# q, k and v projections in 64-row halves, and one pool of 8 PSUM banks, in a transformer block scheduled by a written timetable

## The chip, the cores and the metric

The kernel runs on one core of one Trainium2 chip. The metric is the time of the device in microseconds, from one launch; it is given as the median of a few runs. A profile is one execution recorded by the hardware profiler; its span runs from the first to the last instruction of the program. The engines are called PE (TensorE, matmuls; PEld are its weight loads), DVE (VectorE), ACT (ScalarE), POOL (GpSimd) and SP (SyncE, which issues most DMAs).

## The reference

One block on x of 2048 tokens and 576 features. First a linear-memory attention with 32 heads of 18 features, in four segments of 512 tokens, then a feed-forward part of 4608 hidden features.

```python
xn = layernorm(x)
q, k, v = xn @ wq, xn @ wk, xn @ wv            # 32 heads of 18
for s in range(4):                             # 512 tokens each
    a_dot = softmax(qs @ ks.T * scale + causal_mask) @ vs
    a_mem = (phi(qs) @ M) / (phi(qs) @ z + 1e-6)   # phi(t) = t + 1 if t > 0 else exp(t)
    o = g * a_mem + (1 - g) * a_dot            # g = sigmoid(beta), one for each head
    M, z = M + phi(ks).T @ vs, z + sum(phi(ks))
h = x + o @ wo
out = h + gelu(layernorm(h) @ w1 + b1) @ w2 + b2
```

## The kernel before

The work is written as a graph of some 1,770 operations, each with an engine, a function that issues its instructions, the operations it follows, and the buffers it takes (`acq`) and uses. `Graph.add` gives every operation its place from `TIMETABLE`: a row such as `"P1Pk": "p 174 207 ..."` holds the engine letter and, for each operation of that stage and name in turn, a rank. `Graph.schedule` sorts all operations by rank, picks a buffer number for each acquired buffer with a small cost table, and then issues the operations in that order; each engine carries out its own in order, and waits are made from the data that instructions touch. So the timetable alone decides the order on every engine, and the cost table decides nothing but buffer numbers.

The stages, for segment s:

- X: load 128 tokens of x (two tiles at once from segment 1 on), layer norm on DVE (`stats`, `apply`) with the `rstd` on POOL, and a transpose to `xT` (features on partitions), on PE (`TX`) in segment 0 and by DMA (`flip`) in the others. 576 features are four blocks of 128 and one of 64.
- P: for each of the four tiles of 128 tokens, k, q and v. `proj` (line 743, matmul on line 750) makes one half of the output, 288 columns, in one PSUM bank by five matmuls whose stationary operand is a 128x128 block of `xT` and whose moving operand is 288 columns of the weights; the fifth uses 65 rows. `proj2` (matmul on line 761) makes both halves at once for k and q of the first two tiles. The halves are copied out by ACT or DVE (`copy`), k and q into a padded tile that goes to DRAM (`qkst`) and comes back transposed (`flip`), and `ek`, `rk` and `fk` make phi(k).
- M: the memory update, 32 matmuls on line 852, two additions (`macc`) and the block-diagonal copy (`mblk`).
- A: attention. For two groups of four heads, five score steps (`st`, line 1067; `st0` on line 916 in segment 0), each with 32-row matmuls into four banks at once, an `exp` of 128x2048 on ACT, causal masks on POOL or DVE (`mask`), then the weighted values (`val`, line 1093; line 948 in segment 0) with 32-column matmuls, a DVE transpose and the normalisation (`valT`, `rec`, `comb`). From segment 1 on `mem` (line 1044) reads the memory, with `memT` and `memfin` after it.
- B: the output projection (`Po`, also line 750), the residual (`hadd`), the second layer norm, and a transpose to `x2T`. h goes to DRAM and comes back later (`hc`).
- C: the first feed-forward matmul F1 with 64-row matmuls in pairs, two groups of hidden features side by side (line 1206; 1243 for segment 0, in halves of 256 tokens), copied out with the bias and put through gelu in batches, in segment 3 directly (`gelu1`).
- D: the second feed-forward matmul F2 (line 1293), 36 matmuls of 288 columns into one bank for each of eight outputs of a segment, then the residual (`oadd`) and the store.

A matmul thus comes in four shapes: full (128 rows and columns), 64-row pairs, 32-row fours and 32-column fours.

PSUM has 8 banks of 2 KB for each partition. Before, four of them are the pool `ps_c`, which nearly everything uses. The other four are at first two pairs for `proj2` (`pr`), then, once these are released, the one score tile `st`, and for F1 of segment 3 four single banks (`ps_l`). Since there is one score tile, a score step follows the exp of the score step ahead of it.

SP is a single queue in which the loads of x, of the weights (`w1g`, 576 KB each, three buffers), the stores and the transposes by DMA stand in timetable order.

Of the kernel before, what the change touches and what calls it, by code (L numbers as in the profile page):

```python
# [18 lines left out]
SWITCH = dict(act=1.35, pe=0.1)  # L19
INF = 1e9  # L20
# [276 lines left out]
}  # L297


# [108 lines left out]
def kernel(  # L408
# [12 lines left out]
    P = 128  # L421
# [1030 lines left out]
```

## Time and profile before

| | |
|---|---|
| time, median of 3 runs | 450.41 us (449.86 to 450.85) |
| span of the profiled execution | 448.2 us |
| granted PE clock in it | 1.000 |
| busy in the span: PE, DVE, ACT, POOL | 436.8, 288.7, 300.1, 182.5 us |
| DMA | 76.54 MB, mean 171 GB/s |

The profile does not give the whole time of its execution, only the span. The median of the runs is 2.2 us above it; that difference is taken for what lies around the span.

Rows of groups read: line, engine, operation, output tile <- input tiles, shapes, count | busy us, mean ns of one | idle us of the engine just ahead of them, and what ended it. Matmuls overlap, so the mean of one is its own length and not the distance to the next.

### The profile page before, as it was taken

To read this page: it belongs to the slowest core of one execution; us is meant where nothing else is said; L and a number is where in the kernel's file an instruction comes from. 1 tells how busy PE (TensorE), PEld (TensorE's weight loads), DVE (VectorE), ACT (ScalarE), POOL (GpSimd) and SP (SyncE) were. 2 spreads that over 40 slices of the span, in tenths; PEclk is the share of its full clock that TensorE was granted. 3 is DMA by queue.
4 is the path that set the end of the run, shared out by engine and by line. 5 is a ranking of instruction groups with operands and counts; after the bars stand their busy time and mean duration, and the time that the engine had idled before them with its cause. 6 is when DMAs were issued, how large, how long until landed. Compare 5 with 4: busy or idle time off the path is not lost.

```text
span 448.2 us, 11504 instructions
## 1 busy us (share of the span) xinstructions
PE 436.8 (97%) x4813; PEld 279.9 (62%) x4815; DVE 288.7 (64%) x618; ACT 300.1 (67%) x271; POOL 182.5 (41%) x305
## 2 busy tenths in 40 slices
PE   8978999999999999999999999999999999999997
PEld 4655677776676667664344766655447775445775
DVE  4989899998888877688878879966764011000011
ACT  4888889998887789776999976665766002664000
POOL 4687577447933556743534347432101011000020
PEclk9999999999999999999999999999999999999999
DMA  7799799996979958956663529515460592540020
GB/s 275 198 235 283 204 262 219 260 258 228 227 212 316 331 104 225 242 116 172 206 155 78 143 73 259 107 41 168 113 188 16 148 263 68 187 145 1 0 80 26
DMA packets 81732, 76.54 MB, mean 171 GB/s; under 512 B 59024, under 2 KB 68880, under 8 KB 81680
## 3 DMA queue, kind: packets, MB, share of 16 engines
q1 hardware_dynamic: 81392, 75.59, 61.9%
q8 instruction: 37, 0.61, 0.5%
q10 hardware_dynamic: 288, 0.22, 0.2%
q14 instruction: 15, 0.12, 0.1%
HBM read 42.63 MB, written 19.20 MB: 138 GB/s over the span
## 4 chain that ended last, share of the span: by engine, by line
PE 84%; DVE 8%; POOL 3%; DMA 2%; issue 2%; ACT 0%; SPq 0%; DVEq 0%; POOLq 0%; ACTq 0%
PE ps_c L1293 29%; PE ps_c L1206 16%; PE ps_c L750 13%; PE ps_l L1206 8%; PE ps_c L1243 7%; PE st L1067 4%; PE ps_c L1093 3%; DMA x<-in_A_x_dram 2%; PE ps_c L1044 1%; PE st L916 1%; PE ps_c L948 1%; DVE xn L687 1%; DVE e L1038 1%; DVE t L962 1%; DVE t L1047 1%
## 5 line engine op out<-in xcount | busy, mean ns | idle before, releaser
L1071 ACT ACTIVATE pt<-st 128x2048 bf16<-128x2048 f32 x60 | 112.6, 1877 | 32.1 <-PE st L1067 21.2
L1293 PEld LDWEIGHTS <-hT 128*128 128x128 bf16 x1152 | 111.0, 98 | 33.8 <-issue 5.5
L1206 PEld LDWEIGHTS <-w1g 64*128 64x128 bf16 x972 | 46.6, 94 | 56.5 <-issue 3.2
L1293 PE MATMUL ps_c<-w,hT 128*128 128x288 bf16 x576 | 78.4, 286 | 0.6 <-DVE t L1047 0.6
L1293 PE MATMUL ps_c<-w_lo,hT 128*128 128x288 bf16 x576 | 77.4, 286 | 0.2 <-issue 0.2
L1206 PE MATMUL ps_c<-xreg,w1g 64*128 64x512 bf16 x648 | 72.9, 376 | 0.0
L1305 DVE TENSOR_TENSOR ot<-ps_c,hc 128x288 bf16<-128x288 f32 x32 | 13.7, 448 | 79.1 <-PE ps_c L1293 77.9
L750 PE MATMUL ps_c<-hT,xreg 128*128 128x288 bf16 (+1 forms) x440 | 60.6, 286 | 1.7 <-DVE qk_pad L599 1.4
L1082 POOL TENSOR_SCALAR_AFFINE_SELECT pt<-pt 128x512 bf16<-128x512 bf16 x59 | 42.3, 728 | 39.6 <-ACT pt L1071 39.5
L1211 ACT ACTIVATE hT<-ps_l,b_col 128x512 bf16<-128x512 f32 x36 | 22.7, 684 | 46.2 <-PE ps_l L1206 46.2
L750 PEld LDWEIGHTS <-xreg 128*128 128x128 bf16 (+1 forms) x440 | 40.9, 97 | 16.3 <-issue 5.1
L1279 POOL TENSOR_TENSOR hc<-hc,b_bc 128x576 f32<-128x576 f32 x11 | 14.4, 1309 | 83.1 <-DMA hc<-hd 83.1
L919 ACT ACTIVATE pt<-st 128x2048 bf16<-128x2048 f32 x20 | 37.6, 1878 | 4.7 <-PE st L916 4.3
L1221 DVE TENSOR_SCALAR hT<-ps_c,b_col 128x512 bf16<-128x512 f32 x45 | 32.4, 743 | 11.9 <-PE ps_c L1206 11.9
L1243 PE MATMUL ps_c<-xreg,w1g 64*128 64x256 bf16 x648 | 38.3, 270 | 0.3 <-DVE t L1053 0.3
L1206 PE MATMUL ps_l<-xreg,w1g 64*128 64x512 bf16 x324 | 35.1, 376 | 0.0
L1243 PEld LDWEIGHTS <-w1g 64*128 64x128 bf16 x648 | 30.5, 94 | 6.3 <-issue 2.9
L1226 ACT ACTIVATE hT<-hT 128x8192 bf16<-128x8192 bf16 (+2 forms) x6 | 31.8, 5321 | 0.3 <-DVE hT L1221 0.2
L1219 ACT ACTIVATE hT<-ps_c,b_col 128x512 bf16<-128x512 f32 x27 | 17.9, 685 | 16.5 <-PE ps_c L1206 16.3
L676 POOL TENSOR_SCALAR ln<-ln 128x1 f32<-128x1 f32 x32 | 8.9, 277 | 43.8 <-DVE ln L673 42.5
L1067 PE MATMUL st<-qk 32*128 32x512 bf16 (+3 forms) x384 | 23.8, 301 | 0.0
L750 PE MATMUL ps_c<-wt_o,oT 128*128 128x288 bf16 x160 | 22.7, 286 | 0.0
(114 smaller groups left out, 583.8 us busy)
## 6 DMA issues: line engine op xcount, KB each, us to landing
w1g<-in_B_w_dram SPq DMA_DIRECT2D x42, 576.0 KB, 4.6
qkd<-qk_pad SPq DMA_DIRECT2D x15, 512.0 KB, 3.2
hd<-h SPq DMA_DIRECT2D x16, 288.0 KB, 3.8
hc<-hd SPq DMA_DIRECT2D x16, 288.0 KB, 4.1
w_lo<-in_B_w_dram SPq DMA_DIRECT2D x3, 864.0 KB, 5.5
w<-in_B_w_dram SPq DMA_DIRECT2D x3, 864.0 KB, 7.6
xb<-in_A_x_dram SPq DMA_DIRECT2D x16, 144.0 KB, 3.5
x2d<-xn SPq DMA_DIRECT2D x14, 160.0 KB, 2.0
```

The costliest lines, as they stand in the source:

```text
L750: nc.tensor.matmul(out=c.t[:, 0:HALF], lhsT=xTb.t[0:kk, k, ts], rhs=wt[0:kk, hf, k, :], start=(k == 0), stop=(k == 4))
L919: ex = add(ps, {"act": 1.88}, lambda e: nc.scalar.activation(out=pt.t[:], in_=st.t[:], func=ACT.Exp, scale=scale), [sc], pt, [st], table=" ...
L1067: nc.tensor.matmul(out=st.t[:, i, off:off + n_], lhsT=qk[rows, 1, kt * P:(kt + 1) * P], rhs=qk[rows, 0, kt * P:L], start=True, stop=True, ...
L1071: ex = add(ps, {"act": 1.88}, lambda e, st=st, pt=pt: nc.scalar.activation(out=pt.t[:], in_=st.t[:], func=ACT.Exp, scale=scale), [sc], pt, ...
L1082: nc.gpsimd.affine_select(out=blk, in_=blk, pattern=[[0, 4], [1, P]], compare_op=ALU.is_ge, fill=0.0, base=0, channel_multiplier=-1)
L1206: nc.tensor.matmul(out=cc[w].t[:], lhsT=w1.t[rows, k, q, :], rhs=x2T[s].t[rows, k, :], start=(k == 0), stop=(k == ND - 1))
L1211: ready_f[f + w] = [add(pf - 12, {"act": 0.68}, lambda e, f=f, w=w, cc=cc: nc.scalar.activation(out=hT[:, :, f + w, :], in_=cc[w].t[:].rea ...
L1219: nc.scalar.activation(out=dst, in_=src, func=ACT.Identity, bias=b)
L1221: nc.vector.tensor_scalar(out=dst, in0=src, scalar1=b, scalar2=None, op0=ALU.add)
L1226: ge = add(2.9, {"act": 0.42 * (f1 - f0) + 0.2}, lambda e, f0=f0, f1=f1: nc.scalar.activation(out=hT[:, :, f0:f1, :], in_=hT[:, :, f0:f1, ...
L1243: nc.tensor.matmul(out=cc[w].t[:, q * 2 * P:(q + 1) * 2 * P], lhsT=w1.t[rows, k, q, :], rhs=x2T[s].t[rows, k, ts], start=(k == 0), stop=(k ...
L1293: nc.tensor.matmul(out=c.t[:, 0:HALF], lhsT=hT[:, tl // 2, f, (tl % 2) * P:(tl % 2 + 1) * P], rhs=w2_c[ch][:, f - ch * WCH, hf * HALF:(hf ...
```

## The change

1. `proj` keeps only the output projection. q, k and v go through the new `proj_pair`, which makes both output halves of a tile as three operations: the first part (`Pk`, `Pq`, `Pv`), a fence (`pass`) and the second part (`Rk`, `Rq`, `Rv`). In the first part rows 0 to 63 of the array work on output half 0 and rows 64 to 127 on output half 1, each into its own bank, in five steps; in the second part they change banks and do the remaining four steps. The fence is a memset of a 128x1 tile on DVE or POOL that waits for the last two matmuls of the first part, and the second part's first matmul waits for it. Where the two parts stand next to each other on PE, `schedule` marks them `fused`: then there is no fence, and both halves are made whole by ten matmuls of 128 rows.
2. For this the last 64 features stand twice: x has 640 columns in DRAM, the last 64 repeated, `apply` works on 640, and the fifth block of each weight holds output half 0 in rows 0 to 63 and output half 1 in rows 64 to 127. The memset of the tails of `xn` goes.
3. All 8 PSUM banks are one tile, `bank`. A score step and a `proj2` take four or two neighbouring banks, everything else one; `pick` prefers banks 4 to 7 for single ones.
4. `mem` may be issued as four 32-column matmuls (`alt`), where it stands next to operations of that shape.
5. Buffers: `pt` 5 instead of 4, `t1` 2 instead of 1, `w1` 4 instead of 3. The scratch for dynamic DMA is set to 4096.
6. The whole timetable is new, with some numbers of the cost table. Among the new rows 13 of the 44 `pass` operations are on DVE and 31 on POOL; those of fused pairs issue nothing.

```diff
 class Slots:
-    def __init__(self, tiles):
-        self.tiles = tiles
+    def __init__(self, tiles, whole=None, pref=0):
+        self.tiles, self.whole, self.pref = tiles, whole, pref
...
+    def pick(self, t0):
+        free, w = self.home.free, self.width
+        if self.want is not None:
+            return self.want
+        if w > 1:
+            return min(range(0, len(free), w), key=lambda g: max(free[g:g + w]))
+        ready = [i for i in range(len(free)) if free[i] <= t0] if self.home.pref else []
+        return min([i for i in ready if i >= self.home.pref] or ready or range(len(free)), key=lambda i: free[i])
...
     def schedule(self):
...
+        on_pe = [o for o in order if o.eng == "pe"]
+        for a, b in zip(on_pe, on_pe[1:]):
+            if a.mate is b:
+                a.fused = b.fused = True
...
+            elif op.alt is not None:
+                was = next((o.mode for o in reversed(on_pe[:n]) if o.mode), None)
+                then = next((o.table for o in on_pe[n + 1:] if o.alt is None), None)
+                if was == op.alt or (was != op.mode and then == op.alt):
+                    op.mode = op.alt
...
-    c_s = slots(4, [P, 512], "ps_c", F32, psum)
-    pair_pool, score_pool = ExitStack(), ExitStack()
-    pr_pool = pair_pool.enter_context(tc.tile_pool(name="pairs", bufs=1, space=PSUM))
-    pr_s = slots(2, [P, 2, 512], "pr", F32, pr_pool)
-    st_s = Slots([None])
...
+    banks_all = psum.tile([P, 8, 512], F32, name="bank")
+    c_s = Slots([banks_all[:, j, :] for j in range(8)], banks_all, 4)
...
-        def proj(prio, xTb, tl, nm, hf, after, c):
+        def proj_pair(prio, xTb, tl, nm, after, cc):
             ts = slice(tl * P, (tl + 1) * P)
             wt = wts[nm]
 
+            def rows(w, hf, k, start, stop):
+                r = slice(64 * w, 64 * w + 64)
+                return nc.tensor.matmul(out=cc[hf].t[:, 0:HALF], lhsT=xTb.t[r, k, ts], rhs=wt[r, hf, k, :], start=start, stop=stop, skip_group_check=True)
+            last, passed = [], []
+
+            def fn_f(e):
+                if a.fused:
+                    return
+                passed.append(VEC[e].memset(mark_of[e][:], 0.0))
+                for to in last:
+                    tc.add_manual_dep(passed[0].ins, to.ins.name, SYNC, reason="the two halves of the rows change banks")
+
+            def fn_a(e):
+                if a.fused:
+                    return
+                for k in range(KT):
+                    last[:] = [rows(0, 0, k, k == 0, False), rows(1, 1, k, k == 0, False)]
+
+            def fn_b(e):
+                if not b.fused:
+                    for k in range(KT - 1):
+                        for w in range(2):
+                            i = rows(w, 1 - w, k, False, k == KT - 2)
+                            if k == 0 and w == 0:
+                                tc.add_manual_dep(i.ins, passed[0].ins.name, SYNC, reason="the two halves of the rows change banks")
+                    return
+                for hf in range(2):
+                    for k in range(KT):
+                        nc.tensor.matmul(out=cc[hf].t[:, 0:HALF], lhsT=xTb.t[:, k, ts], rhs=wt[:, hf, k, :], start=(k == 0), stop=(k == KT - 1))
+            a = add(prio, {"pe": 0.613}, fn_a, list(after) + w_ok[nm], cc, [xTb], table="rows64", name="P" + nm)
+            f = add(prio, {"dve": 0.07, "pool": 0.13}, fn_f, [a], name="pass")
+            b = add(prio, {"pe": 0.49}, fn_b, [a, f], None, cc + [xTb], table="rows64", name="R" + nm)
+            a.mate, f.fence = b, a
+            return b
...
-                    for hf in range(2):
-                        c = Buf(c_s)
-                        a = proj(PE_P[s] + 0.001 * tl if s > 1 else p0, xT, tl, nm, hf, [xn_ok[s, tl]], c)
+                    cc = [Buf(c_s), Buf(c_s)]
+                    a = proj_pair(PE_P[s] + 0.001 * tl if s > 1 else p0, xT, tl, nm, [xn_ok[s, tl]], cc)
...
-                st, pt = Buf(st_s), Buf(pt_s)
+                st, pt = Buf(c_s, width=4), Buf(pt_s)
...
-        A_x=a["A_x"],
+        A_x=np.concatenate([a["A_x"], a["A_x"][:, :, 512:]], axis=2),
```

Two rows of the timetable, before and after (ranks run to 1773 before and to 1815 after):

```diff
-    "P2Pk": "p 342 366 411 422 463 529 572 562",
+    "P2Pk": "p 372 424 533 587",
+    "P2Rk": "p 381 433 538 591",
+    "P2pass": "g373 g432 d652 d425 g483 d510 g534 g542 d503 d588 g606 g517",
```

More of the change, by code (lines that the diff above doesn't have):

```diff
@@ L336, in __init__ @@
         self.behind, self.bulk, self.bias, self.tag = None, False, {}, ""
+        self.alt, self.mate, self.fused, self.fence, self.mode = None, None, False, None, table
 class Graph:
@@ L371, in schedule @@
             done.add(op)
+            if op.fence is not None and op.fence.fused:
+                op.start, op.end = op.fence.end, -1.0
+                continue
             t0 = max([free[e]] + [self.seen(a, e) for a in op.after])
             for b in op.acq:
-                b.n = min(range(len(b.home.free)), key=lambda i: b.home.free[i]) if b.want is None else b.want
-                t0 = max(t0, b.home.free[b.n])
-                assert t0 < INF, (op.tag, op.name)
-                b.home.free[b.n] = INF
+                b.n = b.pick(t0)
+                for j in range(b.n, b.n + b.width):
+                    t0 = max(t0, b.home.free[j])
+                    assert t0 < INF, (op.tag, op.name)
+                    b.home.free[j] = INF
             if op.bulk:
@@ L380, in schedule @@
             c = op.cost[e]
-            kind = op.table or ("full" if e == "pe" else None)
+            if op.fused:
+                c = 0.0 if op.mate is not None else FUSED
+            kind = op.mode if e == "pe" else op.table
             if kind is not None and kind != table.get(e):
@@ L396, in schedule @@
                 if b.left == 0:
-                    b.home.free[b.n] = b.end + 0.2
+                    for j in range(b.n, b.n + b.width):
+                        b.home.free[j] = b.end + 0.2
         return order
@@ L506 @@
     mark = const.tile([1, 1], F32, name="mark")
+    mark_of = {e: const.tile([P, 1], F32, name=f"mark_{e}") for e in ("dve", "pool")}
     b1_col = const.tile([P, NF], F32, name="b1_col")
@@ L544 @@
     hd = tc.dram_tile([S, D], F32, name="hd")
-    late_s = Slots([None] * 4)
-    def to_late():
-        if late_s.tiles[0] is None:
-            score_pool.close()
-            pool = ctx.enter_context(tc.tile_pool(name="late_ps", bufs=1, space=PSUM, reuse_waits="tile"))
-            late_s.tiles[:4] = [pool.tile([P, 512], F32, name=f"ps_l{j}") for j in range(4)]
     eps_parts = []
@@ L608, in fn @@
                 for i in range(n):
-                    nc.tensor.matmul(out=acq[i // 2].t[:] if acq else wst.t[:, 0, :], lhsT=warm[:, 0:P], rhs=warm[:], start=True, stop=True)
+                    nc.tensor.matmul(out=acq[i // 2].t[:] if acq else wst.t[:], lhsT=warm[:, 0:P], rhs=warm[:], start=True, stop=True)
             return add(-9, {"pe": cost}, fn, after, acq, use, name="warm")
@@ L612, in build @@
         wprev = warm_up(4, 1.72, [wprev], [Buf(c_s), Buf(c_s)])
-        wprev = add(-9, {"pe": 0.5}, lambda e: [nc.tensor.matmul(out=wst.t[:, 0, :], lhsT=warm[:, 0:P], rhs=warm[:], start=True, stop=True) for _ in range(2)],
+        wprev = add(-9, {"pe": 0.5}, lambda e: [nc.tensor.matmul(out=wst.t[:], lhsT=warm[:, 0:P], rhs=warm[:], start=True, stop=True) for _ in range(2)],
                     [wprev], wst, name="warm")
-        z_xn = memset(-9, "pool", 0.5, *[t[:, D:XW] for t in xn_s.tiles])
         half_ok = memset(-9, "dve", 0.1, mhalf[:], val=-0.5)
@@ L741, in stage_X, with proj, fn @@
                     xn_ok[s, 2 * j] = xn_ok[s, 2 * j + 1] = [prev]
-        def proj(prio, xTb, tl, nm, hf, after, c):
+        def proj(prio, xTb, tl, hf, after, c):
+            ts = slice(tl * P, (tl + 1) * P)
+            def fn(e):
+                for k in range(KT):
+                    nc.tensor.matmul(out=c.t[:, 0:HALF], lhsT=xTb.t[:, k, ts], rhs=wts["o"][:, hf, k, :], start=(k == 0), stop=(k == 4))
+            return add(prio, {"pe": 0.62}, fn, list(after) + w_ok["o"], c, [xTb], name="Po")
@@ L933, in mask @@
                                                     base=0, channel_multiplier=-1)
[L934 removed]
+                    masks[u] = add(ps, {"dve": 0.87, "pool": 1.17}, mask, [ex, tri_ok], None, [pt], name="mask")
                     masks[u].bias = {"dve": MASK_BIAS}
@@ L1041, in stage_A, with mem @@
                 t2s[g] = t2
-                def mem(e, g=g, c=c, eb=eb):
-                    nc.tensor.matmul(out=c.t[:], lhsT=MZ_blk[s - 1][:, g, :], rhs=eb.t[:], start=True, stop=True)
+                def mem(e, g=g, c=c, eb=eb, me=(me := [])):
+                    if me[0].mode == "full":
+                        nc.tensor.matmul(out=c.t[:], lhsT=MZ_blk[s - 1][:, g, :], rhs=eb.t[:], start=True, stop=True)
+                        return
+                    for i in range(4):
+                        nc.tensor.matmul(out=c.t[32 * i:32 * i + 32, :], lhsT=MZ_blk[s - 1][:, g, 32 * i:32 * i + 32], rhs=eb.t[:],
+                                         start=True, stop=True, tile_position=(0, 32 * i), skip_group_check=True)
                 m = add(pg + 0.05, {"pe": 0.22}, mem, [pq, mz_ok[s - 1]], c, [eb], name="mem")
+                m.alt = "cols32"
+                me.append(m)
                 mz_read.setdefault(s, []).append(m)
@@ L1083, in mask @@
                                                     base=0, channel_multiplier=-1)
-                    mk = add(ps, {"dve": 0.46, "pool": 0.68}, mask, [ex] + later, None, [pt], name="mask")
+                    mk = add(ps, {"dve": 0.45, "pool": 0.67}, mask, [ex] + later, None, [pt], name="mask")
                     mk.bias = {"dve": MASK_BIAS}
```

103 lines of the change are left out of this document (46 added, 57 removed), and 556 rows, old and new, of the table TIMETABLE.

## Prediction

> **What bounds the kernel now.** I read the page first: engine shares, then the 40 slices.
>
> ```profile
> span 448.2 us, 11504 instructions
> PE 436.8 (97%) x4813; PEld 279.9 (62%) x4815; DVE 288.7 (64%) x618; ACT 300.1 (67%) x271; POOL 182.5 (41%) x305
> ...
> PE   8978999999999999999999999999999999999997
> PEld 4655677776676667664344766655447775445775
> DVE  4989899998888877688878879966764011000011
> ACT  4888889998887789776999976665766002664000
> ...
> DMA  7799799996979958956663529515460592540020
> ```
>
> TensorE (PE) is taken from end to end; only slices 1 to 4 have gaps. In the first third ACT, DVE and the DMA engines are nearly full too. The windows view (time, then busy time and instructions of PE, PEld, DVE, ACT, POOL) puts sizes on that:
>
> ```profile
> 0.00:40.00 40.00, 33.35 (x438) 22.43 (x439) 31.07 (x75) 29.67 (x42) 27.64 (x56) 1.00 0.91 239
> 40.00:80.00 40.00, 40.00 (x621) 29.09 (x620) 36.73 (x84) 36.12 (x36) 27.79 (x65) 1.00 0.90 233
> 80.00:112.00 32.00, 31.72 (x387) 22.18 (x386) 28.94 (x65) 30.01 (x26) 17.02 (x29) 1.00 0.89 259
> ```
>
> PE idles 6.65 us in the first 40 us, 0.3 in the next 72. So little can be gained by filling gaps after 40 us; the rest must come out of PE's own stream. The chain of waits gives its unit:
>
> ```profile
> 342.18 32.34 PE ps_c L1293 x264
> ```
>
> 32.34 / 264 = 122.5 ns for each matmul of 288 columns without a stop. A single one lasts 286 ns (group row below), so its end comes 164 ns after the next has started. Start times of single matmuls in the trace give the other steps: 216 ns for 512 columns, 109 for a pair of 64-row matmuls of 256 columns (line 1243), 216 for a pair of 512; four 32-row or 32-column matmuls share a step too. Where PE goes from one tile shape to another, the next start is late: at 76.39 us line 1243 gives way to line 750 after 202 ns instead of 109, and over all 211 such places the median is 89 to 96 ns for every pair of shapes; I take 94.
>
> The stream of before in these units: 409.0 us of steps, 212 shape changes x 0.094 = 19.9, first matmul at 1.24, last start to end of span 3.5. 448.2 less these leaves 14.6 us lost, put in place by the single starts: 9.4 in the first 40 us (2.1 of them the 11 warm-up matmuls at 427 instead of 216 ns), 5.2 from 40 to 320, nothing after. The waits view for PE names the losses:
>
> ```profile
> PE ps_c L750 <- DVE qk_pad L599: 1.4, 2, 0.8
> PE ps_c L852 <- DVE fk_pad L828: 1.4, 1, 1.4
> ...
> PE st L916 <- ACT pt L919: 0.6, 1, 0.6
> PE ps_c L1293 <- DVE t L1047: 0.6, 1, 0.6
> PE ps_c L948 <- ACT pt L919: 0.6, 1, 0.6
> ```
>
> **The change, part by part, on the profiled execution (448.2).**
>
> *Halves.* 44 pairs of projections go through `proj_pair`. Whole: 10 matmuls x 122.5 = 1.225 us. In halves: 5 steps of two 64-row matmuls, the fence, 4 steps; 9 x 122.5 = 1.10. But only 16 of the 44 are in halves: the changed program has 288 matmuls of the 64-row form on line 785 (16 x 18) and 280 whole ones on line 811 (28 x 10), since a pair whose two parts stand next to each other on PE is fused. Gain: 16 x 0.1225 = 1.96 us. The 64-row step for 288 columns isn't in the trace; the rows at 256 (109) and 512 (216) put it between, at 122.5.
>
> The Trainium skill, "TensorE: Matmul & The Clock Gate", section "LDWEIGHTS (loading the stationary operand)", speaks against halves: a load takes its columns / 1.2 ns whatever its rows, 107 for 128, and halves need 18 loads for 10; one behind the other, two loads would be 213 ns a step. The trace has 94 ns for the 64-row load, and line 1243, with two such loads a step, still starts a pair every 109 ns, so the two loads of a step overlap there.
>
> ```profile
> L750 PE MATMUL ps_c<-hT,xreg 128*128 128x288 bf16 (+1 forms) x440 | 60.6, 286 | 1.7 <-DVE qk_pad L599 1.4 <-DVE t L962 0.2
> L1243 PEld LDWEIGHTS <-w1g 64*128 64x128 bf16 x648 | 30.5, 94 | 6.3 <-issue 2.9
> L575 DVE MEMSET mhalf<- 128x1 f32 x1 | 0.1, 59 | 0.0
> L932 POOL TENSOR_SCALAR_AFFINE_SELECT pt<-pt 128x1024 bf16<-128x1024 bf16 x15 | 17.0, 1145 | 5.2 <-ACT pt L919 5.2
> ```
>
> *Shape changes.* In the changed order there are 201, not 212: 64-row projections next to F1 or to each other, and 8 of the 24 `mem` matmuls in 32-column form next to `val`. 11 x 0.094 = 1.03 us. Both counts together take PE's stream from 428.9 to 425.9.
>
> *The fence.* Second half waits for `pass` (a 128x1 memset: 59 ns on DVE; 99 to 114 for such memsets on POOL), which waits for the first half's last matmul. Path: 164 ns to that matmul's end, 0.04 to the other engine (the transposes that end at 7.36 release ACT at 7.40), 0.06 to 0.11, 0.05 back (DVE's memset ends at 1.19, PE starts at 1.24): 0.31 to 0.37. What stands between the halves: another half (0.49 to 0.61 us, in 11 of 16), or a score step of 0.22 to 0.33 plus its two shape changes of 0.19, or more. So a free engine makes the fence cost nothing. Without cover it would be 16 x 0.34 = 5.4. But DVE (8 of the passes) and POOL (8) are in-order: behind an instruction in progress the pass waits, and with it everything on PE, since PE is in-order too; next in line on PE are mostly the other pair's second half and then a score that ACT wants. DVE is 92% busy in 40 to 80 us, mean instruction 0.47 us; half of that x 0.92 = 0.21 us; POOL 0.62 x half of 0.60 = 0.19. The cover leaves 0.1 to 0.25 to spare, so I charge 0.08 each: 1.3 us. Bounds: 0, and 8 x 0.88 (`fk`, line 828, stands just before one DVE pass) + 8 x 1.15 (a whole mask before a POOL pass) = 16. I stay near the low end because most passes stand behind instructions that are ready early.
>
> *First 40 us.* Walked by hand with rows of before. The third tile's transposes now stand after the second k projection, not after q: x lands at 7.8, statistics 0.83, rstd 0.8, apply 0.43, so 10.4, while PE is free at 9.65; 0.75 lost instead of the 0.30 and 0.22 there before. The first score stands behind three whole pairs (3.7 us) instead of two halves (1.2): it starts near 18.2, not 15.76, with that work done. ACT then has two copies of 1.01, three more (1.9), the gates (0.22) and the first exp near 19.2 (16.22 before); six exps (11.3), copies (1.6) and `ek` (1.4) bring the last A01 exp to 31.7, against 31.82. PE waits for these exps 0.6 + 0.4 + 0.4 + 1.6 + 1.3 = 4.3 (before 3.4, of which 1.4 for `fk` at `M0M`, which now stands later and finds it done). A02's first score comes at about 35.3 with 26.2 us streamed, before at 36.57 with 27.0: lost 7.9 against 8.3. Carried on to 40 us: 8.5 against 9.4, a gain of 0.9. Bounds: a gain of 4 (warm-ups and first landings stay), a loss of 2.
>
> *One pool of 8 banks, more buffers.* Scores mostly stay on banks 0 to 3 and still alternate with exps; the other four no longer wait for pools to be closed. A fifth `pt`, second `t1`, fourth `w1` buffer loosen waits that are 1.6 us in all after 40 us. The last attention `val` stands at 297.6 us of PE's stream, before at 290.5, so ACT and DVE have 7 us more cover. I take 0.5 of the 5.2; bounds: 2.5 gained, 2.5 lost. The tail is the same: one half tile, 3.5 us; the last h load and its 0.79 add stand 8.8 us of matmuls ahead of the end and need about 7.7.
>
> *Taken at nothing.* The last of five steps uses 128 rows instead of 65: 286 against 288 ns, the same. Rows of x are 640 wide: 0.26 MB more of 76.5, `apply` some 0.05 longer on DVE, and POOL's three memsets of 0.32 together at 2.9 us go; if x lands later for it, the walk above shifts by as much. SP's queue has one load of w1 fewer, and in no 10 us of the stream more than a few issues more or fewer than before.
>
> Sum: 448.2 - 1.96 - 1.03 + 1.3 - 0.9 - 0.5 = 445.1. The runs' median is 450.41, 2.2 above the span, so 447.3.
>
> **Rivals.**
>
> *Fences bind.* Each pass found behind a busy DVE or POOL. For: both are at 53 to 92% there and 14 of the 16 fences fall between 52 and 105 us of the stream, where ACT is at 94% as well. Against: the covers. Without fences the time would be 446.0; slower by over 0.2% (451.3) begins at 5.3 us, 0.33 us lost at each. At 0.4 each: 452.4. Chance 0.09.
>
> *Losses eat the gain.* Losses from 40 to 320 us rise by 2.5 instead of falling by 0.5 because a new order has new late producers (DMA at 0.9 of its time up to 140 us, exps back to back): 447.3 + 3.0 = 450.3. For: three engines and the DMA are nearly full. Against: fewer ACT evictions (76 for 83). Chance 0.14. The same at double size (453), chance 0.03.
>
> *The start gains more.* Scores wait less than in my walk and the first 40 us lose 5.5 rather than 8.5: 444.3. Chance 0.17.
>
> *Weight loads serialize.* Two 64-row loads of 94 ns cost 188 ns a step where 122.5 are streamed: 16 x (9 x 0.188 - 1.225) = 7.5 us more than whole pairs, 456.7. The steps of 109 ns at line 1243 speak against it. This is what the rule quoted above from the Trainium skill would make of it if loads did not overlap. Chance 0.02.
>
> **Numbers.** Forecast case 0.55: 445.5 to 449.4. With the better start, faster has 0.72. A difference under 0.2% (0.9 us) is about what a measurement of this kernel can't tell from none: 449.5 to 451.3, 0.14. Slower: 0.09 + 0.03 + 0.02 = 0.14. The range leaves out the far ends: 443.6 to 451.4.
>
> **What would show it.** Right: 64-row projection pairs every 122 ns; 201 shape changes; PE's idle in the first 40 us near 5.8; second halves starting at once behind their cover. Wrong: first halves' loads 188 ns apart; waits of PE on the `pass` memsets over 2 us in all; or PE's idle from 40 to 320 us above 4, with ACT or a landing as releaser.

## The result, and the profile after

The changed kernel takes 444.87 us (median; 444.52 to 446.06) against 449.86 (449.32 to 450.85) for the kernel before on the same chip: a ratio of 0.9897, 95% interval 0.9879 to 0.9914, so 5.0 us faster. Run again beside the experiments it took 445.20 us, a ratio of 0.9890 (0.9869 to 0.9910). Its times lie in two groups, 444.2 to 444.9 us at a mean granted clock of 0.999 or 1.000, and 445.9 to 446.8 at 0.995 or 0.996, where PE ran for 3.4 us at half its clock; the last section has the rows. The profiled execution (446.06 us, span 444.3) is of the second group.

The page of after, engine shares and two of its rows of 40 slices:

```profile
span 444.3 us, 11828 instructions
PE 435.1 (98%) x4966; PEld 280.6 (63%) x4967; DVE 283.8 (64%) x628; ACT 294.5 (66%) x262; POOL 185.6 (42%) x315
...
PE   8969999999999999999999999999999999999997
...
PEclk9989999999999999999999999999999999999999
```

PE is still the bound, with some 150 more matmuls. The windows view of after (time, then busy time and instructions of PE, PEld, DVE, ACT, POOL; granted clock, DMA share, GB/s):

```profile
0.00:40.00 40.00, 34.74 (x450) 23.52 (x451) 31.58 (x81) 28.89 (x39) 28.39 (x57) 0.96 0.88 227
40.00:80.00 40.00, 39.62 (x672) 28.98 (x670) 36.02 (x86) 36.61 (x34) 28.46 (x64) 1.00 1.06 283
80.00:112.00 32.00, 31.83 (x431) 22.20 (x427) 27.86 (x64) 30.34 (x28) 18.26 (x35) 1.00 1.00 257
```

PE idles 5.26 us in the first 40 us (6.65 before), though part of its busy time there is at half clock; with the same first 40 us at full clock (the run with parted banks, below) it idles 6.21. The waits of PE in after:

```profile
PE bank L1010 <- ACT pt L981: 1.4, 1, 1.4
PE bank L785 <- DVE mark_dve L791: 1.4, 1, 1.4
...
PE bank L978 <- ACT pt L981: 1.2, 2, 0.9
```

The wait for `fk_pad` (1.4) and the two for `qk_pad` (1.4) are gone; a first values step waits 1.4 for an exp, and one fence 1.4 for its memset. No other fence is in the list. The order has 201 shape changes, as counted ahead. Walked by the starts of single matmuls, the span of after is 426.0 us of stream, 9.1 lost in the first 40 us, 4.6 from 40 to 320, and 4.6 ahead of the first matmul and behind the last. Some 1.4 of the 9.1 is the half clock: the run in which only the banks of a later stretch were parted (below) has the same first 40 us at full clock and loses 7.7. So against the kernel before (428.9, 9.4, 5.2):

| term, us | forecast | measured, full clock |
|---|---|---|
| stream (halves and shape changes) | -2.99 | -2.9 |
| fences and start, first 40 us | +1.3 - 0.9 | -1.7 |
| banks and buffers, 40 to 320 us | -0.5 | -0.6 |
| sum | -3.1 | -5.2 |

The stream of both columns is counted from the program with the same lengths of a step and of a shape change, so this row confirms the counts and, with the loads and starts shown further down, the step of 64-row pairs; the 0.094 of a shape change has no experiment that is finer than the scatter.

### The profile page after: what moved, and what is told of

Its sections match the earlier page's. It is cut to its first block, busy times and chain, and to the rows that moved or that the text cites. A ratio compares the mean times of both kernels' runs of the same rounds, so it can differ in the third digit from the quotient of the medians.

```text
span 444.3 us, 11828 instructions
## 1 busy us (share of the span) xinstructions
PE 435.1 (98%) x4966; PEld 280.6 (63%) x4967; DVE 283.8 (64%) x628; ACT 294.5 (66%) x262; POOL 185.6 (42%) x315
## 4 chain that ended last, share of the span: by engine, by line
PE 83%; DMA 4%; POOL 4%; ACT 4%; DVE 2%; issue 2%; ACTq 0%; DVEq 0%; POOLq 0%
PE bank L1360 32%; PE bank L1273 24%; PE bank L811 5%; PE bank L1310 5%; PE bank L776 4%; PE bank L1136 4%; PE bank L785 4%; PE bank L1162 3%; DMA x<-in_A_x_dram 2%; DMA qk<-qkd 2%; ACT pt L981 1%; POOL ln L704 1%; POOL pt L994 1%; ACT pt L1140 1%; ACT hT L1327 1%
## 5 line engine op out<-in xcount | busy, mean ns | idle before, releaser
L1140 ACT ACTIVATE pt<-bank 128x2048 bf16<-128x2048 f32 x60 | 112.5, 1875 | 35.2 <-PE bank L1136 26.4
L1273 PE MATMUL bank<-xreg,w1g 64*128 64x512 bf16 x972 | 107.7, 376 | 0.0
L1360 PE MATMUL bank<-w,hT 128*128 128x288 bf16 x576 | 77.8, 286 | 0.0
L1360 PE MATMUL bank<-w_lo,hT 128*128 128x288 bf16 x576 | 77.5, 286 | 0.0
L1278 ACT ACTIVATE hT<-bank,b_col 128x512 bf16<-128x512 f32 x36 | 22.2, 690 | 47.0 <-PE bank L1273 46.7
L1288 DVE TENSOR_SCALAR hT<-bank,b_col 128x512 bf16<-128x512 f32 x48 | 34.8, 745 | 18.1 <-PE bank L1273 16.9
L981 ACT ACTIVATE pt<-bank 128x2048 bf16<-128x2048 f32 x20 | 37.4, 1876 | 3.8 <-PE bank L978 3.5
L811 PE MATMUL bank<-hT,xreg 128*128 128x288 bf16 x280 | 39.5, 293 | 0.1
L1310 PE MATMUL bank<-xreg,w1g 64*128 64x256 bf16 x648 | 38.2, 269 | 0.0
L811 PEld LDWEIGHTS <-xreg 128*128 128x128 bf16 x280 | 26.6, 100 | 9.7 <-issue 2.6
L1136 PE MATMUL bank<-qk 32*128 32x512 bf16 (+3 forms) x384 | 23.8, 300 | 0.2 <-ACT pt L1140 0.2
L1286 ACT ACTIVATE hT<-bank,b_col 128x512 bf16<-128x512 f32 x24 | 16.0, 685 | 11.9 <-PE bank L1273 11.6
```

The costliest lines, as they stand in the source:

```text
L811: nc.tensor.matmul(out=cc[hf].t[:, 0:HALF], lhsT=xTb.t[:, k, ts], rhs=wt[:, hf, k, :], start=(k == 0), stop=(k == KT - 1))
L981: ex = add(ps, {"act": 1.88}, lambda e: nc.scalar.activation(out=pt.t[:], in_=st.t[:], func=ACT.Exp, scale=scale), [sc], pt, [st], table=" ...
L1136: nc.tensor.matmul(out=st.t[:, i, off:off + n_], lhsT=qk[rows, 1, kt * P:(kt + 1) * P], rhs=qk[rows, 0, kt * P:L], start=True, stop=True, ...
L1140: ex = add(ps, {"act": 1.88}, lambda e, st=st, pt=pt: nc.scalar.activation(out=pt.t[:], in_=st.t[:], func=ACT.Exp, scale=scale), [sc], pt, ...
L1273: nc.tensor.matmul(out=cc[w].t[:], lhsT=w1.t[rows, k, q, :], rhs=x2T[s].t[rows, k, :], start=(k == 0), stop=(k == ND - 1))
L1278: ready_f[f + w] = [add(pf - 12, {"act": 0.68}, lambda e, f=f, w=w, cc=cc: nc.scalar.activation(out=hT[:, :, f + w, :], in_=cc[w].t[:].rea ...
```

## The experiments

All but one start from the changed kernel. None leaves out any of the computation.

**The late fence taken away.** In the timetable one step of segment 0 is moved, so that v of tile 1 is made whole.

```diff
-    "P00Rv": "p 123 132",
+    "P00Rv": "p 123 127",
```

> The one fence that PE waited for in the profile of after (the v projection of the second tile, 1.43 us for the pass on DVE) is taken away: this pair is made whole, the other 15 stay in halves. Theory A (the time is PE's stream plus its waits, and this fence was a wait of its own): the stream hardly changes (425.83 us for 425.89), the 1.5 us go, the exps behind it start some 1.4 us earlier: 443.4 us against 444.9 for after. Rival B (the wait passes on to the next one, the values that wait for the exp): 444.9, with that wait grown from 1.45 to near 3 us.

446.64 us (444.28 to 447.87), ratio 0.9922 (0.9898 to 0.9945). The fence's wait is gone and another stands a little later; timeline of that run:

```profile
24.67 1.39 PE L811 MATMUL bank<-hT,xreg 128*128 128x288 bf16 x10 [0.79 <-DVE v_aug L625]
```

The next pair waits 0.79 us for banks that the same crowded DVE queue empties. The first 40 us lose 7.7 us, as much as with the fence at the same clock. The run's times scatter over 3.6 us, half of them at a mean clock of 0.992. At full clock they are 444.28, 444.82 and 446.33 us, near theory B's 444.9 and not A's 443.4; but the one long wait that B expected, on the values, did not come (1.24 us), several others share it.

**All pairs whole.** `schedule` puts each second part right behind its first.

```diff
+        for o in self.ops:
+            if o.fence is not None:
+                o.start = o.fence.start + 0.2
+                o.fence.mate.start = o.fence.start + 0.4
         order = sorted(self.ops, key=lambda o: o.start)
```

> All 44 pairs whole, everything else of the new order kept; the work that stood between two halves now stands behind the pair. Steps 408.96 us for 407.00, 195 shape changes for 201: stream 427.29 us for 425.89. Theory A: 1.4 us more stream and 1.5 us less wait at the first fence, so 444.8, and 1.5 above the kernel with one pair made whole. Rival C (the halves give nothing, what they save goes into waits for fences that no row names): no more than the kernel with one pair whole, 443.4 or below.

446.97 us (446.32 to 447.75), ratio 0.9933 (0.9920 to 0.9947), an interval that does not touch that of the changed kernel. Without halves the rest of the change still brings 0.7%; the halves bring 1.8 us of the 5.0 (446.97 less 445.20, the changed kernel run again), of which 1.3 is stream (427.3 against 426.0). Taken at like clock the medians differ by 2.1 us at full clock (446.65 and 444.53, both series of the changed kernel together) and by 1.4 at 0.995 and 0.996 (447.33 and 445.95). Theory A's 444.8 was too low: it counted the 1.5 us of the late fence, which is gone here too, as a gain, and that gain did not come. Rival C (443.4 or below) is out.

**A slow fence.** Three memsets of 128x128 instead of one of 128x1.

```diff
-    mark_of = {e: const.tile([P, 1], F32, name=f"mark_{e}") for e in ("dve", "pool")}
+    mark_of = {e: const.tile([P, 128], F32, name=f"mark_{e}") for e in ("dve", "pool")}
...
+                for _ in range(2):
+                    passed[0] = VEC[e].memset(mark_of[e][:], 0.0)
```

> Each pass is three memsets of 128x128 instead of one of 128x1, about 0.45 us longer on DVE and 0.5 on POOL. The prediction's cover leaves 0.1 to 0.25 us to spare at each fence, so each of 16 should lose 0.2 to 0.35: 3.2 to 5.6 us, 448.1 to 450.5. If the covers are longer than I took them for, or PE's loss is made good at later waits, under 446.

451.99 us (451.89 to 452.94), ratio 1.0052 (1.0040 to 1.0064): slower than before, and above the 450.5 that was expected at most. All five executions had a clock of 0.991 to 0.996, so 1.2 to 1.7 us of it may be the half clock; against the changed kernel at such a clock (445.95) it is 6.0 us. Its waits of PE:

```profile
PE bank L785 <- DVE mark_dve L795: 3.7, 7, 2.1
PE bank L785 <- POOL mark_pool L795: 2.0, 5, 0.5
```

PE now waits at 12 places for a pass, and the loss between 40 and 120 us rises from 2.1 to 6.1 us. So the covers are short: the fence of the changed kernel is free because its pass is short and finds its engine free, not because there is much work between the halves.

**`mem` in full shape only.**

```diff
-                m.alt = "cols32"
```

> The 8 memory reads in 32-column form go back to full shape; 207 shape changes for 201, steps unchanged. Theory A: 6 x 0.094 = 0.57 us more, 445.4. Rival B (such places stand in front of a wait that takes it up): 444.9.

446.68 us (444.75 to 447.89), ratio 0.9926 (0.9902 to 0.9951); 444.75 and 445.06 at full clock, where the changed kernel has 444.2 to 444.9. Six shape changes more should be 0.56 us; the scatter is as large, so this shows no more than that the term isn't big.

**The changed kernel again**, for the comparison with the next three:

> The changed kernel, unaltered, for a comparison on the same chip as the next three. Theory A (the scatter of its times is a stretch of half clock that sets in at about 30.6 us when PE has idled enough before it): its runs fall in two groups, 444.5 to 444.9 at a mean clock of 0.999 or 1.000 and 445.6 to 447.9 at 0.996 or less, nothing between 444.9 and 445.6 at full clock. Rival B (the scatter is of something else): runs above 445.5 appear at clock 1.000 too.

445.20 us (444.20 to 446.84). The times at full clock were 444.20 to 444.54, those at 0.995 and 0.996 were 445.86 to 446.84: the two groups of theory A. (The run with idle matmuls, below, has 446.04 at full clock too, so the half clock is not all of the scatter.)

**The instruction in front of the late pass moved behind it.**

```diff
-    "X1apply": "d 72 85 116 114",
+    "X1apply": "d 72 85 128.5 114",
```

> One rank: the third layer-norm apply of tile 1 of X (DVE, 1.47 us at 22.94 us) goes from rank 116 to 128.5, behind the first pass (126); the halves stay. Theory A (the first fence was late only because of what was queued ahead of it on DVE): the wait of 1.43 us on that pass falls below 0.3 us, the time that PE loses in the first 40 us falls from 9.1 by 1.0 to 2.4 us (the upper figure if the half clock of 31 us goes too), every run has a clock of 0.999 or more, and the median is 443.0 to 443.9. Rival B (the start is bound by something behind the fence, as in the run with that pair whole): the wait moves to the evictions, the exps or the scores' banks, the time lost falls by under 0.5 us, and the median is 444.3 to 445.5.

444.95 us (444.80 to 445.34), ratio 0.9884 (0.9867 to 0.9900). The fence costs nothing any more, as theory A has it, but the median is that of theory B. Timeline:

```profile
28.05 0.40 PE L978 MATMUL bank<-qk 32*128 32x128 bf16 x16 [1.62 <-DMA qk<-qkd]
...
30.44 0.61 PE L978 MATMUL bank<-qk 32*128 32x128 bf16 x16 [1.18 <-ACT pt L981]
```

PE comes to the first of these score steps early and waits 1.62 us for its transposes by DMA, which it did not wait for when it came late; the values in between no longer wait.

The median hides a difference of clock. Three of the four executions had a clock of 0.995 or 0.996, against theory A, and took 444.80, 444.81 and 445.34 us, where the changed kernel at that clock took 445.86 to 446.84: about 1 us less. In the profiles, both of them with one stretch of half clock, the loss in the first 40 us is some 0.5 us smaller than in after and the span 0.7 (443.6 for 444.3). The one execution at full clock took 445.08, which is no less than the changed kernel's 444.20 to 444.87. So part of the fence's wait may well be gained here; four executions do not settle it.

**More halves.** Ten ranks are moved so that 28 of the 44 pairs are in halves instead of 16, for example

```diff
-    "P2Pk": "p 372 424 533 587",
+    "P2Pk": "p 368 424 533 587",
```

> Twelve more of the 44 pairs in halves (28 instead of 16): 405.53 us of matmul steps and 200 shape changes at 0.094, a stream of 424.3 instead of 426.0. Theory A (a pair in halves saves one step of 122 ns, and a pass with work between the halves costs nothing): 1.6 us less than the changed kernel at the same clock, 442.9 to 443.3 at full clock, waits on passes in the stretch from 40 us on under 0.3 us in all. Rival B (the twelve were left whole because their covers are too short): waits on passes of over 1.5 us in all behind 40 us, and 444.5 us or more at full clock.

451.95 us (449.50 to 453.93), ratio 1.0033 (1.0016 to 1.0051): slower than before; at full clock 449.5 and more. The stream is 1.6 us shorter, 424.3 us, but the profiled span is 447.8 at a clock of 1.000, so 18.9 us are lost (447.8 less 424.3 and the 4.6 around) where the changed kernel loses 12.3. Timeline:

```profile
20.64 1.15 PE L785 MATMUL bank<-hT,xreg 64*128 64x288 bf16 x16 [1.53 <-DVE mark_dve L791]
...
33.28 2.26 PE L785 MATMUL bank<-hT,xreg 64*128 64x288 bf16 x34 [0.52 <-POOL mark_pool L791]
```

These two fences hold PE for 2.05 us, more than all twelve pairs save; but the late fence of the changed kernel, 1.43 us there, costs nothing here, so that the waits on passes grow by 1.1 us in all (2.5 for 1.4). Behind 40 us they are 0.4 us in one wait, where theory B wanted over 1.5. Yet the loss between 40 and 120 us goes from 2.1 to 6.2 us, in gaps of 0.2 to 0.6 around halves, scores and memory steps. So B's time came, but not by its mechanism; the moved steps also hold their banks longer and shift what stands behind them, and which of it costs the 4 us was not separated.

**Idle matmuls in a wait.** Ten matmuls, overwritten later, in front of the first values step.

```diff
+                fill = 10 if not v0_read else 0
...
+                    for _ in range(fill):
+                        nc.tensor.matmul(out=banks[units[0][0] // 2].t[:, 0:HALF], lhsT=wts["v"][:, 0, 0, 0:P], rhs=wts["v"][:, 0, 0, :],
+                                         start=True, stop=True, skip_group_check=True)
```

> Ten idle matmuls (288 columns, their result overwritten) in front of the first values step, where PE waits 1.45 us on the exp: 1.22 us of the wait becomes busy, nothing else changes. Theory A (the half clock at 31 us follows PE's idle time of the 8 us before it): all runs at a clock of 0.999 or more, 444.5 to 444.9 us, no stretch at half clock. Rival B (the drop has another cause, the work that starts there or chance): runs at 0.996 and below stay as frequent as in the changed kernel, with 445.6 us and more.

445.42 us (444.54 to 446.04), ratio 0.9892 (0.9874 to 0.9910), a clock of 0.999 or 1.000 in all five executions, as theory A has it, though the time reaches 446.04 and its median is 0.9 us above that of the changed kernel at full clock (444.53). Where 5 executions of 11 of the changed kernel had the half clock, none in five still comes by chance about one time in ten. Timeline:

```profile
28.70 1.39 PE L1007 MATMUL bank<-hT 128*128 128x288 bf16 x10 [1.45 <-ACT pt L981]
30.02 0.85 PE L1014 MATMUL bank<-pt,v_aug 128*19 128x128 bf16 x48
```

The expectation was wrong on one point: the idle matmuls, which read nothing that the exp writes, wait for it all the same. They write the bank of the values step and share nothing else with the exp, so it must be that bank, with the scores of the exp in it, that comes free no sooner than the operand; the trace has no bank numbers to show it. The filler took the place of the next wait (0.92 us, on the score step) instead.

**The score step behind the pair that follows it.**

```diff
-    "A01exp": "a 130 154 166 158",
+    "A01exp": "a 130 154 171.7 158",
...
-    "A01st0": "p 129 143 161 153",
+    "A01st0": "p 129 143 171.5 153",
```

> One step moved: the fourth scores step of the first segment (rank 161, at 30.99 us behind a wait of 0.92 us on an exp) and its exp go behind the first k pair of tile 0 of X1 (rank 171); one more shape change (0.094 us). Theory A (how late PE leaves the start is set by the flip of X1, issued at 24.6 to 24.7 us and landing 5.8 us later, and by what stands on PE ahead of the pair that needs it, so that a fence wait of 1.43 us at 23 us costs next to nothing): the pair starts at 30.3 to 30.6 us instead of 31.2 to 31.5, the scores wait no more, and at full clock the time is 443.3 to 444.0 us (the changed kernel: 444.2 to 444.9). Rival B (the exps pace the start, so that scores moved later cost as much as they free): the wait comes back within 10 us, and the time at full clock is 444.3 to 445.5 us.

445.57 us (445.06 to 446.12), ratio 0.9899 (0.9884 to 0.9913). Timeline:

```profile
30.80 1.40 PE L811 MATMUL bank<-hT,xreg 128*128 128x288 bf16 x10 [1.18 <-DMA xreg<-xnd]
...
34.56 1.39 PE L811 MATMUL bank<-hT,xreg 128*128 128x288 bf16 x10 [0.70 <-ACT pt L981]
```

Half of each theory: the first pair of segment 1 now waits for the flip of X1 and starts as it lands (issued at 25.0, 5.8 to landing), but what is won there is given back 4 us later to a bank that an exp frees. The first 40 us lose 8.3 us. All four executions were at full clock, and they are slower than the changed kernel's there (444.20 to 444.87), so theory A's time (443.3 to 444.0) is out.

**The same, and the flip one place earlier on SP.**

```diff
-    "X1flip": "s 148 219",
+    "X1flip": "s 143.5 219",
```

> As the run before, and the flip of X1 on SP goes ahead of the write of q and k of tile 1 (0.51 us of issue at 24.07 us). Theory A (the flip's landing paces PE): it lands about 0.6 us earlier, at 29.7 to 29.9 us, PE's first pair of X1 starts by 30.1 us, and at full clock the time is 442.9 to 443.7 us. Rival B (nothing is waiting for the flip): the first pair starts where it did, and the flips of q and k of tile 1, issued 1.6 us later, make scores at 35 us wait: 444.3 us or more.

445.15 us (445.08 to 445.86), ratio 0.9893 (0.9878 to 0.9907). The flip lands at 29.5 (25.2 and 4.3) and the pair starts with no wait:

```profile
30.04 1.40 PE L811 MATMUL bank<-hT,xreg 128*128 128x288 bf16 x10
...
33.81 1.39 PE L811 MATMUL bank<-hT,xreg 128*128 128x288 bf16 x10 [0.71 <-ACT pt L981]
```

0.76 us sooner than in the run before, and the time falls by 0.4 us at most; it is no better than that of the changed kernel, all four executions again at full clock. A score step ahead of the pair, at 28.52 us, now waits 1.24 us. 7.9 us are lost in the first 40 us.

**The kernel before without its longest wait.** Its first memory step, which waits 1.38 us for `fk_pad`, is moved.

```diff
-    "M0M": "p 156 224",
-    "M0macc": "d 159 248",
+    "M0M": "p 169.3 224",
+    "M0macc": "d 169.6 248",
```

> The kernel before, with its first memory step (rank 156, which waits 1.38 us for fk_pad at 29.4 us) and its addition moved to ranks 169.3 and 169.6, as the new timetable has the memory steps later; halves, banks and buffers as before. Theory A (the new order, by itself, takes a wait out of the start): the wait for fk_pad is gone, the first 40 us lose 1.0 to 1.5 us less, and the median is 448.5 to 449.1 us, 1.0 to 1.5 below the kernel before. Rival B (the start is paced by the flip of X1, which lands at 31.65 us here, so that a wait in front of it costs nothing): the median is 449.6 to 450.3 us.

449.73 us (449.47 to 452.10) against 449.88, a ratio of 1.0001 (0.9989 to 1.0013): nothing. Timeline:

```profile
30.05 0.41 PE L916 MATMUL st<-qk 32*128 32x128 bf16 x16 [1.32 <-ACT pt L919]
```

The score step that comes up instead waits 1.32 us for the exp that frees its one tile.

**Banks parted again, for one stretch.** For steps that the timetable's reckoning puts between 120 and 200 us, `pick` gives banks 0 to 3 to scores alone and 4 to 7 to single ones. (The pool was not parted all through, and neither were one `t1` or four `pt` tried: no run shows what the pool or the buffers are worth alone.)

```diff
         if w > 1:
-            return min(range(0, len(free), w), key=lambda g: max(free[g:g + w]))
+            return min(range(0, len(free), w) if len(free) != 8 or not 120 < t0 < 200 else range(0 if w == 4 else 4, 4 if w == 4 else 8, w), key=lambda g: max(free[g:g + w]))
+        if len(free) == 8 and 120 < t0 < 200:
+            return min(range(4, 8), key=lambda i: free[i])
```

> The changed kernel with the pool of 8 banks parted as before for the steps that the timetable's own reckoning puts between 120 and 200 us: scores in banks 0 to 3 alone, single banks from 4 to 7 alone; order and halves the same. Theory A (the common pool is worth what was charged for it, 0.5 us over 280 us, so about 0.15 here): 444.3 to 445.2 us at full clock, and PE's time lost between 120 and 200 us rises from 1.45 to at most 1.9 us. Rival B (the new order lives on the common pool): over 3.5 us lost there, 446.5 us or more.

448.04 us (446.31 to 450.25), ratio 0.9954 (0.9934 to 0.9975), 446.3 to 447.5 at full clock. Its waits of PE have two that no other run of the changed kernel has, both on the output projection:

```profile
PE bank L778 <- DVE h L1215: 1.1, 1, 1.1
...
PE bank L778 <- DVE t L1118: 0.8, 1, 0.8
```

They stand at 164 and 166 us, and the loss between 160 and 180 us goes from 0.1 to 2.3 us. That is on the side of theory B (446.5 us or more; over 3.5 lost between 120 and 200 us): with this order, parting the pool over this one stretch costs 2.2 us.

## Why the prediction was right, and where it was not

The time, 444.87 for 447.3, is inside the range (443.6 to 451.4), but 0.6 us below the band of the forecast case (445.5 to 449.4). Of that case, PE's stream shrank as forecast; the fences cost less and the start lost less, and this surplus is nearer to the rival "the start gains more". The gain was 5.0 us where 3.1 was forecast, and the difference, some 2 us, is all in the first 40 us (7.7 lost for 9.8). The steps one by one:

*Halves and shape changes: right.* All 288 matmuls of 64 rows are there. Timeline of after around the second fence:

```profile
57.44 0.78 PE L785 MATMUL bank<-hT,xreg 64*128 64x288 bf16 x10
58.15 0.40 PE L978 MATMUL bank<-w_lo 32*128 32x128 bf16 x16
58.48 0.66 PE L785 MATMUL bank<-hT,xreg 64*128 64x288 bf16 x8
```

The first row is five pairs, the second the score step that covers the fence, the third the second half. Of the first row, 0.78 less the 0.283 of one matmul is four steps of 0.124. The loads (query of line 785):

```profile
L785 PEld LDWEIGHTS <-xreg x288: 92/94/96, 22.4 to 117.4; 64*128 64x128 bf16 x144
```

Two loads of 94 ns a step, and still 124 ns from step to step: they overlap. That answers the rule weighed in the prediction, the Trainium skill, "TensorE: Matmul & The Clock Gate", section "LDWEIGHTS (loading the stationary operand)": the length of a load hardly falls with the rows (94 ns for 64, 97 to 100 for 128, where the formula gives 107), as it says, but two row groups load side by side, and the rival in which they follow one another falls.

*The fences: the step that failed.* I charged 1.3 us as 0.08 for each. Fifteen cost PE nothing: their pass begins 0 to 0.08 us after the first half's last matmul ends (one 0.25), and the second half follows its cover without a gap, as in the three rows above. I had each pass come upon a busy engine as the share of busy time has it; but the new order puts the pass where its engine stands ready. In 7 of the 16 places the engine had already sat idle and waited for PE, 9.5 us in all (query of line 791, what its engine idled for):

```profile
  PE bank L785: 9.5, 7
```

The sixteenth pass, the first in time, comes late and costs 1.43 us, because DVE has a layer-norm apply that waits for POOL's `rstd`, and evictions, in front of it:

```profile
22.94 1.47 DVE L715 TENSOR_SCALAR xn<-x,ln 128x640 bf16<-128x640 bf16 x1 [0.46 <-POOL ln L704]
24.33 0.94 DVE L625 TENSOR_SCALAR v_aug<-bank,ln 128x288 bf16<-128x288 f32 x2
24.77 0.06 DVE L791 MEMSET mark_dve<- 128x1 f32 x1
...
24.91 0.66 PE L785 MATMUL bank<-hT,xreg 64*128 64x288 bf16 x8 [1.43 <-DVE mark_dve L791]
```

As a sum that is the 1.3 I had. But I added it to the end of the kernel, and the runs do not show that it arrives there: without that fence (first experiment; all pairs whole too) the time at full clock is no shorter than that of the changed kernel, since other waits come up in its place. Without its lateness (sixth) the executions at 0.995 and 0.996 are about 1 us shorter and the one at full clock is not, so how much of the 1.43 counts stays open. An average of 0.08 was the wrong form as well: in this trace a pass is either free or behind something that itself waits.

*The first 40 us: too small a gain.* Forecast 8.5 lost, with the fences on top 9.8; measured 7.7 at full clock, the 1.43 included. The hand walk had five waits on exps, 4.3 us; the trace has the two large ones (1.45 and 0.92 for 1.6 and 1.3), and the three small ones did not come. One cause of the wide miss is that I priced waits one at a time: in this stretch the landing of X1's flip (30.5 us), the exps on ACT and the banks that they free end within about a microsecond of each other, and each wait taken away in the experiments came back as another, in whole or in great part. The loss stays between 7.7 and 8.3 us at full clock in four such kernels. The new order, the pool and the buffers together brought it from 9.4 to 7.7; which of them, and which moves of the order, I have not separated, so the cause of this gain stays open. Removing the `fk` wait from the kernel before, which I had counted as 1.4 of its 3.4, gave nothing.

*Banks and buffers: right in size, wrong in kind.* 4.6 us lost from 40 to 320 for a forecast 4.7, an agreement that owes something to chance: the 0.5 was a guess between 2.5 gained and 2.5 lost. It is not what the pool is worth. Parting it over one stretch costs 2.2 us: the new order leans on it there, and the two were not priced apart.

*The rivals.* "Fences bind" needed 0.33 us at each fence, and the slow fence shows that this price was near: at three longer memsets the kernel is slower than before. "Losses eat the gain" did not come with 16 halves; with 28 the losses from 40 us on did rise by more than its 2.5. "The start gains more" (444.3) is nearest to the time measured, with its mechanism half right: the start lost 7.7 us, its one late fence included, where the forecast makes 9.8 with the fences and this rival 6.8 (5.5 and 1.3).

No kernel tried here has a median below the changed one's by more than the runs scatter.

## What to carry to other kernels

A term such as a fence is to be priced by its single places: look at which instruction stands in front of it on its engine, and whether that one itself waits. Where several chains end close together, as at the start here, do not count on the length of a wait as what its removal gains: of the four removed here, three gained nothing that the runs can tell, and the fourth perhaps 1 us. Count on the stream, and price waits there as a group. More of a good thing needs its own trial: 16 pairs in halves gained 1.4 to 2.1 us, 28 were some 5 us slower than those 16, though the passes themselves cost little more. And compare executions at like clock before two medians are compared.

## What the runs showed of the hardware

PE fell to half its clock in the middle of the kernel, after waits of no more than 1.5 us. Windows of after (the last three columns are granted clock, DMA share, GB/s):

```profile
30.00:32.00 2.00, 1.08 (x27) 0.72 (x20) 1.90 (x6) 1.80 (x3) 1.92 (x4) 0.69 1.10 355
32.00:34.00 2.00, 2.00 (x10) 1.29 (x9) 1.24 (x6) 1.88 (x2) 1.74 (x6) 0.50 1.38 249
```

In windows of 0.1 us the half clock lasts from 30.77 to 34.18 us, 3.41 us; in the second profile of the same kernel from 31.17 to 34.59, 3.42 by such windows; in the run with `mem` in full shape from 30.28 to 37.11, twice that. The Trainium skill, "TensorE: Matmul & The Clock Gate", section "What's actually happening", has the clock decided by the activity in free-running windows of 3413 ns that do not start with the kernel. The lengths agree with that, and so does it that one execution of a kernel has the stretch and the next has not. But its advice in "Why this matters for your kernels", to avoid idle gaps of more than about 3 us, is too mild for this case: here two waits of 1.45 and 0.92 us within 3.4 us were enough, in 5 of 11 executions. With the wait that follows filled by idle matmuls none of five had it; the kernel before, with 0.55 and 1.38 us, 3 of 49.

How the two waits fall into stretches of 3.41 us fits better than their lengths. By the record of the clock in the trace of after, it first comes up at 6.88 us, and the half clock begins seven such stretches later. In the run with the score step moved, which waits 1.25 and 1.18 us and showed no half clock in four executions, the stretches begin at 5.03 us. The stretch with the most idle time of PE, in after:

```profile
27.35:30.77 3.42, 1.23 (x61) 0.96 (x61) 3.35 (x9) 3.42 (x2) 3.29 (x5) 1.00 1.09 180
```

and in the run with the score step moved:

```profile
25.51:28.92 3.41, 1.83 (x52) 1.13 (x54) 3.34 (x11) 2.82 (x4) 3.11 (x7) 1.00 0.99 192
```

In the first, one stretch holds both waits and PE is busy for 1.23 us; the half clock follows. In the second the two waits fall into two stretches, and neither has PE busy for less than 1.83 us. Of the six profiles with a half clock, five have 1.14 to 1.24 us busy in the stretch ahead of it; in the eight without, no stretch has less than 1.83. The sixth, `mem` in full shape only, has 1.89 ahead of its half clock and does not fit. So the place of the waits in the stretches would explain why one execution drops and the next does not, but with one profile in fourteen against it the rule stays open.

The price is 1.2 and 1.7 us between the two groups of times of the changed kernel (445.97 less 444.81, 445.95 less 444.26), about a quarter to a third of what the whole change gained; half the clock over 3.41 us would be 1.7. In the run with the apply moved, two of the three executions with it were shorter than the one without. The half clock makes the time of the changed kernel scatter more than that of the kernel before. (The run with idle matmuls scatters by 1.5 us at full clock, so it is not the only reason.)
